# Moving state copies, routing's parts, the gate reduction and the first loads in the attention stage of a fused kernel

## The chip, the cores and the metric

The kernel runs on one core of a Trainium2 chip. A core has five engines, each with its own instruction queue that runs in order: TensorE (PE; its weight loads are shown as PEld), VectorE (DVE), ScalarE (ACT), GpSimd (POOL) and SyncE (SP, which only issues transfers here). Transfers run on 16 DMA engines. The metric is device time in microseconds from the first to the last instruction of one execution, with what lies around it; lower is better.

## The reference, cut to what matters

Three blocks follow one another on B = 4 sequences of S = 576 rows of 512 numbers: a retention (causal attention with a decay per head and no softmax), a mixture of eight experts with one expert for each row, and a Fourier block with a feed-forward part.

```python
ret = (q @ k.T) / 8 * Dmat            # Dmat = gamma_h ** (row - column), causal
x = ret @ v                           # (4, 576, 512), eight heads of 64
logits = x @ w_gate                   # (4, 576, 8)
local = sigmoid(x @ w_local)          # under 0.5, or at row 0: take the row's own argmax, else keep the last expert
out[b, s] = p[e] * (relu(x[b, s] @ w1[e]) @ w2[e])
u = x + real(fft2(x)); out = u + relu(norm(u) @ w_ch1) @ w_ch2
```

## The kernel before, in words

The change lies in the first stage, `attention`, and in two places of `fused_kernel` and `layouts` that feed it. The rows are cut into 18 steps (`STEPS`): for each of four blocks of 128 rows (c = 0 to 3) the four sequences one after the other, so step i = 4c + b, and then two steps for the last 64 rows of two sequences each (c = 4). All engines run an order that is written out by hand: the order of the Python calls is the order of each engine's queue.

What belongs to one step:

- `load(i)`: two transfers on SP's queue, q and k transposed (`qk`, 512 KB) and k and v (`vk`, 512 KB). There are three `qk` buffers and four `vk` buffers, so `load(i + 3)`, issued in step i, waits for the last reader of `qk(i)`.
- `prep(i)`, issued in step i - 2, on POOL: `qg`, q times its decay (c > 0), then `ks`, k times its decay (c < 4; two buffers).
- `scores(i)`: TensorE's state products `sp` from `ks` and v (c < 4; one PSUM bank, `st`); VectorE copies them into `total` (c = 0) or adds the earlier state; with c = 3 ScalarE copies the sum into `apart` in two halves (`sb`). Then TensorE's scores `a`, and VectorE's two products with the decay table `dec`, which make `am`.
- `outputs(i)`, in step i + 1: TensorE's products of state and `qg`, and of v and `am`, into `o`; ScalarE copies them to `xT`.
- `back(i)`, in step i + 1: TensorE multiplies `xT` by `idw`, the identity with the nine gate columns, into the one bank `tr`. VectorE sums the gates' part over the four blocks (`L`, L527). ScalarE takes the sum of magnitudes (`Abs`, L536, with a read-out), VectorE makes a scale of it in three small operations (L537 to L546), ScalarE writes the scaled row's fp16 high half (`xh`, L547), VectorE the low half (`xl`, L549). The bank is then free for the next `tr`.
- `route(c)`: for each block of four steps, a generator of four parts: maximum, differences `ls`, choice, and ScalarE's exponential `ex`; then a transposition, the normaliser (`rate`, L582 to L585) and a scan along the rows; then the choice turned back; then ranks by TensorE, the gate, and the slots at which rows go to their expert. `turn` advances every live generator once a step. After the last part, `scatter` sends rows by an indirect transfer on POOL's queue, two a step.
- `beside(i)`: work on the weights of expert 0, whose eight pieces `w.load(j)` brings (512 KB each, issued by `hook`): `absmax(j)` on ScalarE in step j + 6, `high(j)` on ScalarE and `low(j)` on VectorE in steps 11 and later.

A step's calls in order: `outputs(i - 1)`, first part of `beside`, `scores(i)`, `tr` and gates, second part of `beside`, `Abs` to `xh`, third part of `beside`, `prep(i + 2)`, `load(i + 3)`, `level` (the decay table of the next block, every fourth step), `turn`, `xl`, `scatter`, the first part of a new `route` (i = 4, 8, 12, 16), `hook`. After step 17 come the first half of an expert's products, the last routing, the scatter of the last rows, and the loads of the second expert's weights, whose number the routing has just found.

Of the kernel before, what the change touches and what calls it, by code (L numbers as in the profile page):

```python
# [20 lines left out]
E, FF = 8, 2048  # L21
# [20 lines left out]
WARM = 15  # L42
FILLED = 4
# [302 lines left out]
def attention(keep, tc, nc, A, xs, rows, hook, beside, after, sizes, zeros, first, spare, hid0, mt0):  # L346
# [19 lines left out]
    def load(i):  # L366
# [61 lines left out]
    def prep(i):  # L428
# [4 lines left out]
        if c > 0:  # L433
            qg = wk.tile([128, 4, 128], FP32, tag="qg", name="qg", bufs=3)
            for j in range(len(lanes)):
                w = slice(n * j, n * j + n)
                nc.gpsimd.tensor_tensor(out=qg[:, :, w], in0=qT[:, :, w], in1=qds[c][:, :, 0:n], op=ALU.mult)
        if c < 4:
            ks = wk.tile([128, 512], FP32, tag="ks", name="ks")
            h8 = lambda t: t.rearrange("p (h d) -> p h d", h=H)  # L440
            nc.gpsimd.tensor_tensor(
                out=h8(ks), in0=h8(k), in1=kd[:, c, :].unsqueeze(2).to_broadcast([128, H, D]), op=ALU.mult
            )
        pre[i] = (qg, ks)

    def scores(i):
# [27 lines left out]
        pair = [p2.tile([128, 4, 128], FP32, tag="a", name="a") for _ in range(2)]  # L474
        for j in range(len(lanes)):
            w = slice(n * j, n * j + n)
            for p in range(4):
                for g, a in enumerate(pair):
                    r = slice(64 * g, 64 * g + 64)
                    nc.tensor.matmul(out=a[w, p, 0:n], lhsT=kT[r, p, w], rhs=qT[r, p, w], start=True, stop=True)  # L480
        for g, a in enumerate(pair):
            for j in range(len(lanes)):
                w = slice(n * j, n * j + n)
                V.tensor_tensor(out=m[w, g::2, 0:n], in0=a[w, :, 0:n], in1=dec[w, g::2, w], op=ALU.mult)
# [33 lines left out]
    def back(i):  # L518
# [6 lines left out]
        if i % 4 == 0:  # L525
            L[c] = rt.tile([128, 4, 9], FP32, tag="L", name="L", bufs=2)
        V.tensor_reduce(  # L527
            out=L[c][:, i % 4, :], in_=tr[:, :, 128:137].rearrange("p a e -> p e a"), axis=AX.X, op=ALU.add
        )
# [6 lines left out]
        nc.scalar.activation(out=xh.bitcast(BF16), in_=tr, func=ACTF.Abs, accum_out=mx[:, 0:1])  # L536
        V.tensor_scalar(  # L537
# [8 lines left out]
        V.reciprocal(out=mx[:, 2:3], in_=pi)  # L546
        nc.scalar.activation(out=xh, in_=tr, func=ACTF.Copy, scale=mx[:, 2:3])  # L547
# [3 lines left out]
    def route(c):  # L551
# [89 lines left out]
        V.tensor_tensor(out=gate[:, at], in0=ps, in1=sm, op=ALU.mult)  # L641
        c8 = W("c8", [128, 2, 8])
# [77 lines left out]
    live = []  # L720

    def turn():
        for g in list(live):
            if next(g, "end") == "end":
                live.remove(g)

    level(1)
    for i in range(N):
# [7 lines left out]
        scores(i)  # L736
# [40 lines left out]
    next(early[3])  # L777
    next(r, None)
# [1439 lines left out]
def fused_kernel(tc, A, out, stop=None):  # L2218
    nc = tc.nc
    with ExitStack() as ctx:  # L2220
# [5 lines left out]
        with tc.manual_schedule():  # L2226
# [51 lines left out]
            def hook(i):  # L2278
                w = weights(0)
                if i == 0:  # L2280
# [12 lines left out]
                if 2 <= i < 10:  # L2293
                    w.load(i - 2)
# [69 lines left out]
def layouts(q, k, v, moe_w_gate, moe_w_local, moe_w1, moe_w2, moe2_w_ch1, moe2_w_ch2):  # L2364
# [3 lines left out]
    for i, lanes in enumerate(STEPS):  # L2368
# [10 lines left out]
        "w_gate": c(moe_w_gate),  # L2379
        "w_local": c(moe_w_local),  # L2380
# [24 lines left out]
```

## Time and profile before

| | |
|---|---|
| runs shown | 790.6, 798.08, 790.78 us; median 790.78 |
| profiled execution | 787.88 us, span 785.7 us |
| busy in the span | PE 724.8 (92%), PEld 542.8, DVE 592.3 (75%), ACT 411.8 (52%), POOL 126.8 us |
| DMA | 142.27 MB, mean 181 GB/s |
| mean granted clock of TensorE | 0.988 |
| attention's steps | from 7.7 to about 112 us |

Times in the rows below count from the span's start. A line such as L524 is a line of the kernel before. In a timeline, "[1.58 <-ACT xT L516]" says that the engine stood idle for 1.58 us before the instruction, and what ended that. A busy engine need not be the one that sets the end: within a stage, what counts is which wait ends last.

### The profile page before, as it was taken

The numbers are of one execution on the slowest core, as the hardware profiler recorded it, in microseconds if no ns is written. First come the engines' busy times: TensorE is split into PE (matmuls) and PEld (weight loads), VectorE is DVE, ScalarE is ACT, GpSimd is POOL, SyncE is SP. The second block draws the span as 40 slices with busy tenths as digits, with TensorE's granted clock in tenths as the row PEclk, the third lists the DMA queues.
The fourth block names the chain that finished last, engine by engine and source line by source line (L and its number), as shares of the span: only waits on it lengthen the run. The fifth ranks groups of instructions, "written<-read, shape, count | busy, mean of one in ns | idle before, by whom it ended". The sixth has DMA issues, their size and how long they took to land. (4 is left out here: it accounts for less than half of the span.)

```text
span 785.7 us, 17150 instructions
## 1 busy us (share of the span) xinstructions
PE 724.8 (92%) x6529; PEld 542.8 (69%) x6529; DVE 592.3 (75%) x1432; ACT 411.8 (52%) x829; POOL 126.8 (16%) x225
## 2 busy tenths in 40 slices
PE   8888898899999998879998999899899999999996
PEld 5677685655566555557644448778788888888885
DVE  3678888589889988857898969958876695646462
ACT  1356657378888797845847526426332451414140
POOL 3566443002102201113000011010010001010101
PEclk9999999899999999999999999999999999999998
DMA  9998449999998998964427276600550017110000
GB/s 296 355 305 293 154 115 309 295 315 344 293 360 304 270 352 287 262 235 149 136 77 240 102 214 232 175 28 2 170 150 2 28 62 195 28 55 2 28 2 27
DMA packets 91929, 142.27 MB, mean 181 GB/s; under 512 B 48116, under 2 KB 49017, under 8 KB 90814
## 3 DMA queue, kind: packets, MB, share of 16 engines
q1 hardware_dynamic: 87246, 126.78, 51.4%
q0 software_dynamic: 4592, 14.31, 5.0%
q8 instruction: 53, 0.87, 0.4%
q14 instruction: 38, 0.31, 0.1%
HBM read 97.55 MB, written 35.12 MB: 169 GB/s over the span
## 5 line engine op out<-in xcount | busy, mean ns | idle before, releaser
L1666 PE MATMUL g<-gxt,wh 128*128 128x256 f16 (+1 forms) x992 | 143.6, 284 | 2.6 <-DMA gxt<-un 1.4
L2011 PEld LDWEIGHTS <-hd 128*128 128x128 f16 x1176 | 114.2, 98 | 26.9 <-issue 7.1
L1666 PEld LDWEIGHTS <-wh 128*128 128x128 f16 x1056 | 102.8, 98 | 28.5 <-issue 4.9
L286 DVE SCALAR_TENSOR_TENSOR wl<-wst,ws,wh 128x1024 f16<-128x1024 f32 (+1 forms) x82 | 100.3, 1253 | 8.1 <-ACT wh L281 8.0
L281 ACT ACTIVATE wh<-wst,ws 128x1024 f16<-128x1024 f32 x80 | 89.0, 1140 | 26.1 <-DVE ws L274 25.7
L815 PE MATMUL ps<-xt,wh 128*128 128x320 f16 (+4 forms) x544 | 79.1, 284 | 8.1 <-DMA xt<-xs 5.8
L845 PE MATMUL ps<-wh,hid 128*128 128x512 f16 (+2 forms) x528 | 84.6, 302 | 0.2 <-ACT hid L831 0.2
L2011 PE MATMUL g<-wh,hd 128*128 128x256 f16 x448 | 78.3, 273 | 4.3 <-DVE u L2040 2.0
L1666 PE MATMUL g<-gxt,wl 128*128 128x256 f16 (+1 forms) x496 | 80.5, 285 | 0.0
L815 PEld LDWEIGHTS <-wh 128*128 128x128 f16 x640 | 57.5, 100 | 33.2 <-issue 13.8
L1872 POOL DMA_INDIRECT out<-u,orow x18 | 17.9, 993 | 383.9 <-DVE u L2040 284.8
L845 PEld LDWEIGHTS <-hid 128*128 128x128 f16 (+2 forms) x792 | 46.4, 100 | 42.4 <-issue 2.7
L239 ACT ACTIVATE wh<-wst 128x1024 bf16<-128x1024 f32 x66 | 69.3, 1050 | 7.7 <-DVE wst L311 5.2
L2040 DVE SCALAR_TENSOR_TENSOR u<-g,ffs,u 128x256 f32<-128x256 f32 (+1 forms) x63 | 34.1, 568 | 49.3 <-PE g L2011 48.7
L1982 DVE SCALAR_TENSOR_TENSOR s<-g,r 128x256 f32<-128x256 f32 x168 | 53.3, 374 | 23.4 <-ACT hd L1976 22.7
L1955 ACT ACTIVATE hd<-s 128x640 f16<-128x640 f32 x56 | 41.3, 737 | 47.8 <-DVE s L1982 47.8
L1975 ACT ACTIVATE r<-g 128x256 f32<-128x256 f32 x56 | 21.1, 378 | 84.0 <-PE g L1666 78.0
L2011 PE MATMUL g<-e,hd 128*128 128x256 f16 x504 | 59.9, 273 | 5.0 <-DVE u L2040 4.0
L859 POOL DMA_INDIRECT x<-y,mt x25 | 31.5, 1261 | 194.7 <-ACT y L857 149.7
L2011 PE MATMUL g<-wl,hd 128*128 128x256 f16 x224 | 61.1, 273 | 0.0
L1666 PEld LDWEIGHTS <-wl 128*128 128x128 f16 x528 | 51.9, 98 | 11.7 <-issue 1.1
L845 PE MATMUL ps<-wl,hid 128*128 128x512 f16 (+2 forms) x264 | 56.4, 302 | 0.0
(299 smaller groups left out, 1280.7 us busy)
## 6 DMA issues: line engine op xcount, KB each, us to landing
wst<-in_moe_w SPq DMA_DIRECT2D x64, 512.0 KB
raw<-in_ch SPq DMA_DIRECT2D x14, 1024.0 KB
qk<-in_qkv SPq DMA_DIRECT2D x18, 512.0 KB
vk<-in_qkv SPq DMA_DIRECT2D x16, 512.0 KB
pair<-ch SPq DMA_DIRECT2D x32, 256.0 KB
ch<-d SPq DMA_DIRECT2D x14, 512.0 KB
wst<-ch SPq DMA_DIRECT2D x14, 512.0 KB
u<-u SPq DMA_DIRECT2D x9, 512.0 KB
```

Of the source, the lines that this page charges most:

```text
L239: self.nc.scalar.activation(out=x, in_=t, func=ACTF.Abs, accum_out=self.am[:, j : j + 1])
L281: self.nc.scalar.activation(out=self.dst[0][:, j, :], in_=self.pieces[j], func=ACTF.Copy, scale=self.by(j))
L286: self.nc.vector.scalar_tensor_tensor(out=l[:, j, c], in0=self.pieces[j][:, c], scalar=self.by(j), in1=h[:, j, c], op0=ALU.mult, op1=ALU.s ...
L815: nc.tensor.matmul(out=ps, lhsT=m[:, k, 128 * f : 128 * f + 128], rhs=xt[:, x + k, :], start=(k == 0 and i == 0), stop=(k == 3 and i == last),
L845: nc.tensor.matmul(out=ps[r * j : r * j + r, 0:d], lhsT=hid[x][:, f, 128 * t : 128 * t + r], rhs=m[:, 4 + f // 2, c : c + d], start=(f == ...
L859: nc.gpsimd.indirect_dma_start(out=x2[:, :].rearrange("t (k d) -> (t k) d", k=k), out_offset=bass.IndirectOffsetOnAxis(ap=mt, axis=0), in_ ...
L1666: nc.tensor.matmul(out=ps, lhsT=m[:, k + 4 * (f // 8), 128 * (f % 8) : 128 * (f % 8) + 128], rhs=xt[x][:, k, :], start=(k == 0 and i == 0) ...
L1955: nc.scalar.activation(out=hd[:, 0, 2:7], in_=s, func=ACTF.Copy, scale=C2 / 2)
L1975: nc.scalar.activation(out=r, in_=p[:, 1:3], func=ACTF.Relu)
L1982: V.scalar_tensor_tensor(out=d, in0=x, scalar=0.0, in1=y, op0=ALU.max, op1=op)
L2011: nc.tensor.matmul(out=ps, lhsT=hid[k][:, y, x, :], rhs=E[w][m][k], start=(k == 0 and m == y == 0), stop=(k == 7 and y == 1),)
L2040: V.scalar_tensor_tensor(out=y, in0=p, scalar=fs[:, c : c + 1], in1=y, op0=ALU.mult, op1=ALU.add)
```

## The change

- `scores`: the scores `a` and `am` come first, then `sp`; the copy of the state (c = 0) goes from VectorE to ScalarE and, with the `sb` copies, into `keep_state`, called behind the row's `xh`.
- `back`: the gates' reduction comes behind `Abs` (but for the last row), and `xh` becomes a part of its own, behind the third part of `beside`.
- `route`: the first part (c < 3) runs in the following step behind its scores; the second and fourth part are cut in two (c < 3) by `yield "amid"`, and what follows the cut runs behind `xl`.
- `prep`: `ks` ahead of `qg`.
- Loads: `kd` between the halves of load 0; `idn` and one array `gates` (for `w_gate` and `w_local`) ahead of load 1, and `idw` made by a copy on ScalarE instead of a broadcast transfer; `cb`, `rt` and `pos` in step 1; `level` a step earlier; the zero fill in step 3 instead of 0 and the pieces of expert 0 in steps 4 to 11 instead of 2 to 9.
- `WARM` 15 to 9, `FILLED` 4 to 5.

The diff, cut to its core:

```diff
-WARM = 15
-FILLED = 4
+WARM = 9
+FILLED = 5
...
-    load(0)
-    kd = const("kd", [128, 4, 8], src=A["kd"].rearrange("p (c h) -> p c h", c=4))
+    kd = const("kd", [128, 4, 8])
+    load(0, lambda: nc.sync.dma_start(out=kd, in_=A["kd"].rearrange("p (c h) -> p c h", c=4)))
     dec = const("dec", [128, H, 128], src=A["dec"].rearrange("p (h q) -> p h q", h=H))
+    idw, idn = const("idw", [128, 4, 137]), keep.tile([128, 128], FP32, name="idn")
+    nc.sync.dma_start(out=idn, in_=A["idn"])
+    nc.sync.dma_start(out=idw[:, :, 128:137], in_=A["gates"].rearrange("p (c e) -> p c e", c=4))
+    nc.scalar.copy(out=idw[:, :, 0:128], in_=idn.unsqueeze(1).to_broadcast([128, 4, 128]))
     load(1)
...
-    idw = const("idw", [128, 4, 137])
-    nc.sync.dma_start(out=idw[:, :, 0:128], in_=A["idn"].unsqueeze(1).to_broadcast([128, 4, 128]))
-    nc.sync.dma_start(out=idw[:, :, 128:136], in_=A["w_gate"].rearrange("(c p) e -> p c e", p=128))
-    nc.sync.dma_start(out=idw[:, :, 136:137], in_=A["w_local"].rearrange("(c p) e -> p c e", p=128))
...
+    def rest():
+        for t, n in ((cb, "cb"), (rtab, "rt"), (pos, "pos")):
+            nc.sync.dma_start(out=t, in_=A[n])
...
-            if c == 0:
-                V.tensor_copy(out=total[b][0], in_=sp)
-            else:
+            if c > 0:
                 V.tensor_tensor(out=total[b][c % 2], in0=sp, in1=total[b][(c - 1) % 2], op=ALU.add)
-            if c == 3:
-                for g in range(2):
+            def keep_state():
+                if c == 0:
+                    nc.scalar.copy(out=total[b][0], in_=sp)
+                for g in range(2) if c == 3 else ():
                     r = slice(64 * g, 64 * g + 64)
                     nc.scalar.copy(out=apart[b][r, :, r], in_=total[b][1][r])
...
         nc.scalar.activation(out=xh.bitcast(BF16), in_=tr, func=ACTF.Abs, accum_out=mx[:, 0:1])
+        if i < N - 1:
+            logits()
...
         V.reciprocal(out=mx[:, 2:3], in_=pi)
+        yield
         nc.scalar.activation(out=xh, in_=tr, func=ACTF.Copy, scale=mx[:, 2:3])
...
         if c < 4:
             rate()
+        if c < 3:
+            yield "amid"
...
         V.tensor_tensor(out=gate[:, at], in0=ps, in1=sm, op=ALU.mult)
+        if c < 3:
+            yield "amid"
...
-        scores(i)
+        kept = scores(i)
+        for g in fresh:
+            next(g)
+        live.extend(fresh)
+        fresh.clear()
...
         next(r, None)
         next(more, None)
+        next(r, None)
+        kept()
         if i + 2 < N:
             prep(i + 2)
         if i + 3 < N:
             load(i + 3)
-        if i % 4 == 1 and 2 <= i // 4 + 2 <= 4:
-            level(i // 4 + 2)
+        if i % 4 == 0 and i < 16:
+            level(i // 4 + 1)
+        if i == 1:
+            rest()
         turn()
         next(r, None)
+        turn(amid)
+        amid.clear()
...
-            live.append(route(i // 4 - 1))
-            next(live[-1])
+            if i < 16:
+                fresh.append(route(i // 4 - 1))
+            else:
+                live.append(route(i // 4 - 1))
+                next(live[-1])
...
-                if i == 0:
+                if i == 3:
...
-                if 2 <= i < 10:
-                    w.load(i - 2)
+                if 4 <= i < 12:
+                    w.load(i - 4)
```

## Rows read from the trace of the kernel before

**Rows 1.** Stages: length; busy PE, PEld, DVE, ACT, POOL; clock, DMA share, GB/s

```profile
13.74:28.94 15.20, 12.78 (x171) 10.68 (x169) 8.89 (x24) 5.56 (x12) 4.39 (x4) 1.00 0.99 304
28.94:35.33 6.39, 4.81 (x75) 4.24 (x73) 4.51 (x12) 2.08 (x5) 4.29 (x4) 1.00 1.03 419
35.33:41.47 6.14, 4.96 (x74) 4.36 (x74) 5.11 (x18) 2.90 (x6) 2.86 (x4) 1.00 1.02 373
41.47:51.43 9.96, 9.88 (x153) 8.89 (x153) 7.17 (x29) 5.85 (x12) 4.88 (x7) 1.00 0.96 324
51.43:57.24 5.81, 4.78 (x73) 4.22 (x73) 4.03 (x14) 2.17 (x7) 5.25 (x11) 1.00 0.86 255
57.24:63.95 6.71, 4.95 (x73) 4.35 (x74) 5.71 (x16) 3.89 (x8) 4.38 (x8) 1.00 1.01 396
68.77:98.74 29.97, 25.08 (x388) 22.05 (x386) 26.55 (x89) 20.73 (x41) 16.29 (x29) 1.00 0.54 165
98.74:112.07 13.33, 12.84 (x175) 11.30 (x176) 11.94 (x44) 7.39 (x15) 5.22 (x16) 1.00 0.41 122
```

**Rows 2.** Timeline, first steps: start, length, engine, line, operation, out<-in

```profile
1.79 5.13 PE L717 MATMUL warm<-z 128*128 128x512 f16 x15 [1.79 <-POOL z L2272]
...
10.94 1.04 POOL L441 TENSOR_TENSOR ks<-vk,c_kd 128x512 f32<-128x512 f32 x1 [3.31 <-DMA vk<-in_qkv]
```

**Rows 3.** Timeline around routing's first and second part, T4 and T5

```profile
33.23 1.26 POOL L437 TENSOR_TENSOR qg<-qk,qd 128x512 f32<-128x512 f32 x1 [1.41 <-DMA qk<-in_qkv]
33.42 1.12 DVE L560 TENSOR_TENSOR ls<-L,m 128x32 f32<-128x32 f32 x1
...
34.71 0.57 ACT L516 COPY xT<-o 128x512 f32<-128x512 f32 x1
...
35.33 1.21 PE L524 MATMUL tr<-c_idw,xT 128*128 128x137 f32 x8 [1.58 <-ACT xT L516]
...
41.47 1.18 PE L524 MATMUL tr<-c_idw,xT 128*128 128x137 f32 x8 [1.18 <-DVE xr L549]
```

**Rows 4.** Waits up to 115 us: us in total, times, the longest

```profile
ACT xr L536 <- DVE L L527: 25.5, 16, 3.1
...
ACT xT L516 <- PE o L509: 9.9, 1, 9.9
...
PE sp L458 <- POOL ks L441: 3.0, 3, 1.2
```

**Rows 5.** Groups of instructions up to 112 us: count, busy, mean ns, idle before

```profile
L484 DVE TENSOR_TENSOR am<-a,c_dec 128x512 f32<-128x512 f32 x32 | 20.5, 680 | 2.8 <-PE a L480 2.8
L549 DVE SCALAR_TENSOR_TENSOR xr<-tr,mx,xr 128x512 f16<-128x512 f32 x17 | 12.7, 747 | 7.2 <-ACT xr L547 7.1
L286 DVE SCALAR_TENSOR_TENSOR wl<-wst,ws,wh 128x1024 f16<-128x1024 f32 x4 | 5.1, 1278 | 0.0
L468 DVE TENSOR_TENSOR sum<-sp,sum 128x256 f32<-128x256 f32 x12 | 4.9, 412 | 0.1
...
L583 DVE TENSOR_SCALAR sm<-sm 128x4 f32<-128x4 f32 x4 | 3.1, 784 | 0.1
...
L565 DVE TENSOR_REDUCE fr<-t 128x4 f32<-128x32 f32 x4 | 0.7, 186 | 0.1
...
L547 ACT ACTIVATE xr<-tr,mx 128x512 f16<-128x512 f32 x17 | 11.7, 687 | 13.5 <-DVE mx L546 8.4 <-DVE oh L605 3.1 <-DVE sm L582 2.0
L536 ACT ACTIVATE xr<-tr 128x512 bf16<-128x512 f32 x17 | 10.2, 598 | 25.6 <-DVE L L527 25.5
...
L281 ACT ACTIVATE wh<-wst,ws 128x1024 f16<-128x1024 f32 x8 | 9.0, 1143 | 0.0
...
L472 ACT COPY sb<-sum 64x256 f32<-64x256 f32 x8 | 3.2, 401 | 1.4 <-DVE sum L468 1.3
```

**Rows 6.** Timeline: piece 7's magnitude; the second expert's loads

```profile
80.02 1.06 ACT L239 ACTIVATE wh<-wst 128x1024 bf16<-128x1024 f32 x1
...
116.47 3.75 SPq L229 DMA_DIRECT2D wst<-in_moe_w  x6
```

More of the change, by code (lines that the diff above doesn't have):

```diff
@@ L364, in attention, with load @@
     loads = {}
-    def load(i):
+    def load(i, amid=lambda: None):
         lanes = STEPS[i]
@@ L371, in load @@
         nc.sync.dma_start(out=qk.rearrange("p x c s -> p (x c s)"), in_=A["qkv"][i, :, 0:1024])
+        amid()
         nc.sync.dma_start(
@@ L432, in prep @@
         qg = ks = None
[L433 to L437, printed above, removed]
         if c < 4:
@@ L443, in prep @@
             )
+        if c > 0:
+            qg = wk.tile([128, 4, 128], FP32, tag="qg", name="qg", bufs=3)
+            for j in range(len(lanes)):
+                w = slice(n * j, n * j + n)
+                nc.gpsimd.tensor_tensor(out=qg[:, :, w], in0=qT[:, :, w], in1=qds[c][:, :, 0:n], op=ALU.mult)
         pre[i] = (qg, ks)
@@ L451, in scores @@
         am[i] = m = wk.tile([128, H, 128], FP32, tag="am", name="am")
+        pair = [p2.tile([128, 4, 128], FP32, tag="a", name="a") for _ in range(2)]
+        for j in range(len(lanes)):
+            w = slice(n * j, n * j + n)
+            for p in range(4):
+                for g, a in enumerate(pair):
+                    r = slice(64 * g, 64 * g + 64)
+                    nc.tensor.matmul(out=a[w, p, 0:n], lhsT=kT[r, p, w], rhs=qT[r, p, w], start=True, stop=True)
+        for g, a in enumerate(pair):
+            for j in range(len(lanes)):
+                w = slice(n * j, n * j + n)
+                V.tensor_tensor(out=m[w, g::2, 0:n], in0=a[w, :, 0:n], in1=dec[w, g::2, w], op=ALU.mult)
         b, c = lanes[0]
@@ L464, in scores @@
                 )
-            if c == 0:
-                V.tensor_copy(out=total[b][0], in_=sp)
-            else:
+            if c > 0:
                 V.tensor_tensor(out=total[b][c % 2], in0=sp, in1=total[b][(c - 1) % 2], op=ALU.add)
-            if c == 3:
-                for g in range(2):
+            def keep_state():
+                if c == 0:
+                    nc.scalar.copy(out=total[b][0], in_=sp)
+                for g in range(2) if c == 3 else ():
                     r = slice(64 * g, 64 * g + 64)
                     nc.scalar.copy(out=apart[b][r, :, r], in_=total[b][1][r])
[L474 to L484, printed above, removed]
+            return keep_state
+        return lambda: None
     def outputs(i):
@@ L526, in back, with logits @@
             L[c] = rt.tile([128, 4, 9], FP32, tag="L", name="L", bufs=2)
-        V.tensor_reduce(
-            out=L[c][:, i % 4, :], in_=tr[:, :, 128:137].rearrange("p a e -> p e a"), axis=AX.X, op=ALU.add
-        )
+        whole = tr
+        def logits():
+            V.tensor_reduce(
+                out=L[c][:, i % 4, :], in_=whole[:, :, 128:137].rearrange("p a e -> p e a"), axis=AX.X, op=ALU.add
+            )
+        if i == N - 1:
+            logits()
         yield
@@ L536, in back @@
         nc.scalar.activation(out=xh.bitcast(BF16), in_=tr, func=ACTF.Abs, accum_out=mx[:, 0:1])
+        if i < N - 1:
+            logits()
         V.tensor_scalar(
@@ L719, in attention, with turn @@
     prep(1)
[L720 to L724, printed above, removed]
+    live, fresh, amid = [], [], []
+    def turn(of=None):
+        for g in list(live if of is None else of):
+            said = next(g, "end")
+            if said == "end":
                 live.remove(g)
-    level(1)
+            if said == "amid":
+                amid.append(g)
     for i in range(N):
@@ L777, in attention @@
     next(early[3])
+    next(r, None)
     next(r, None)
@@ L2378, in layouts @@
         "qkv": qkv.reshape(len(STEPS), 128, 2048),
-        "w_gate": c(moe_w_gate),
-        "w_local": c(moe_w_local),
+        "gates": c(
+            np.concatenate([moe_w_gate, moe_w_local], axis=1).reshape(4, 128, E + 1).transpose(1, 0, 2).reshape(128, 4 * E + 4)
+        ),
         "moe_w1": c(moe_w1),
```

8 lines of the change are left out of this document (3 added, 5 removed).

## The prediction

> **What bounds the kernel now.** I read four views in this order: busy time by stage, the timeline of the first 115 us, the list of waits, and the groups of instructions with their mean times. The change touches only the attention stage. It consists of 18 steps, and I mark step i+1 by the start of the `tr` matmuls of row i, called T(i): T0 is 13.74, T3 28.94, T4 35.33, T5 41.47, T7 51.43, T8 57.24, T9 63.95, T10 68.77, T15 98.74, T17 112.07.
>
> The stage has three limits one after the other. Up to T4 the DMA engines are full (shares 0.99 and 1.03) while TensorE works 12.78 of 15.20 us [rows 1]; the matmuls `sp` wait for `ks`, 3.0 us in three waits, and `ks` waits for its load [rows 2, 4]. From T5 to T7 TensorE is full: 9.88 of 9.96 us, so about 4.9 us a step is its floor [rows 1]. Four other intervals lie above it: T3 to T4 6.39, T4 to T5 6.14, T7 to T8 5.81, T8 to T9 6.71 [rows 1]. All four are routing's. In the first and third, `ex` stands on ScalarE ahead of the copy `xT` and waits for VectorE's `ls`, so `tr` starts 1.58 us late, "ACT xT". In the second and fourth, routing's second part stands on VectorE ahead of the low part `xl`, and `tr`, whose only bank `xl` frees, starts 1.18 us late, "DVE xr" [rows 3]. From T10 to T15 (29.97 us for five steps) VectorE is busy 26.55 us: nearly full [rows 1]. So a removed wait is worth its length before T10 and little after it.
>
> What the stage gains reaches the end: the second expert's weight loads are issued at 116.47 [rows 6], after the routing has named that expert, and the DMA engines are at a share of 0.41 from T15 to T17 [rows 1], so no transfer begun earlier holds them. I pass gains on one for one.
>
> **The start.** `kd` goes between the two halves of load 0; `idn` (64 KB) and one merged `gates` transfer (18 KB) go ahead of load 1, and a 256 KB broadcast, `cb`, `rt`, `pos`, the first `qd` and the 1.1 MB of zero fill go behind load 3 or later. At the 304 GB/s of the stage [rows 1] the 82 KB put `ks(1)`, now at 10.94 [rows 2], off by 0.3 us, to 11.2. After it come 1.04 us of `ks` and some 0.7 us of `sp`; the scores `a` of step 1 no longer stand behind `sp`. T0 becomes 13.0. For steps 1 to 3 TensorE needs 12.78/3 = 4.26 us [rows 1] and some 0.2 of gaps. The new loop on ScalarE is as long: `xh` 0.69, the state copy now on ScalarE, 0.4 by its neighbour `sb`, `xT` 0.57, `tr` 1.2, `Abs` with its read-out 0.75, and 0.75 for VectorE's three small operations with their hand-overs [rows 3, 5], together 4.4. I take 4.53, so T3 = 13.0 + 13.6 = 26.6 against 28.94: **-2.3**. Loads do not prevent it: loads 0 to 4 with their constants are 6.1 MB, which at 304 GB/s are there at about 23, and `sp(4)` wants `ks` at 25. Bounds: 0 if the loads come as late as now, -3.0 at TensorE's 4.26.
>
> WARM 15 to 9: the fifteen ran 1.79 to 6.92 [rows 2], and nothing waits for the six; what could lose is the clock, at most the 2 us that the first `a`, `sp` and `o` would take longer. I take 0. The copy that makes `idw` lies on ScalarE before its first `xT`, where it idles 9.9 us [rows 4]. FILLED changes nothing: no row is ready before step 7. `rest` is 0.18 MB and its first reader is step 5. `level` one step earlier is wanted two steps later.
>
> **Steps 4 and 8.** Routing's first part leaves the end of the step and comes after the next scores. `xT` has nothing ahead of it, and the step falls to TensorE's 4.9: 6.39 - 4.9 and 5.81 - 4.9, **-2.4**. Bounds: 0 if `xT` finds another instruction ahead, -2.6 at 4.8.
>
> **Steps 5 and 9.** They now hold the first part (five operations of some 0.2 us [rows 5]), `ex`, the normaliser (`rate`, four operations), then `xl`, and only then the rest of the second part. Counted from `tr`: `am` ends at 0.7, `sum` at 1.1, the maximum at 1.3. Then `ls`, and here VectorE meets GpSimd: `ls` took 1.12 us, from 33.42 to 34.54, beside a `qg` that ran 33.23 to 34.49; and `L583` took 0.78 in the mean though it has four numbers a row [rows 3, 5]. In the new order `ks(i+2)` can begin when `sp(i)` has given its buffer back, at 0, and `qg` follows to 2.4. So `ls` ends at 2.4, `ex` at 2.7, `Abs` with its read-out at 3.45, the three small operations with hand-overs at 4.1, `xh` at 4.85, `xl` at 5.6, and the next `tr` at 5.8. 6.14 - 5.8 and 6.71 - 5.8: **-1.25**. Without a meeting `xl` ends at 4.65 and TensorE's 4.9 to 5.0 binds, -2.85; if `rate` meets both GpSimd operations too, 6.6, and the sum is +0.35.
>
> The Trainium skill says why (SBUF — State Buffer, "Who interferes with whom"): the second port pair is an exclusive lock, and whichever of a VectorE operation with two SBUF inputs and a GpSimd operation that reads SBUF starts first holds it to its end. The 1.12 us agrees. It speaks against moving the first part to where `qg` runs; by the rule alone the step is 5.8 and the sum the one below, without it 5.0 and 1.6 us less.
>
> **Gates behind magnitudes.** `Abs` now waits for the gates' reduction `L527`, 25.5 us in 16 waits [rows 4]. Reversed, it starts 0.2 us earlier, but the reduction then waits for `Abs` and stands ahead of the three small operations: 0. If it fitted inside the read-out, -0.2 for each of nine steps (1 to 3, 5, 9, 12 to 15), -1.8.
>
> **Steps 11 to 17.** In steps 12 to 15 the two `sb` copies (0.8 us) leave a gap ahead of `Abs` and go between `xh` and the next `xT`. The `high` of 1.14 us, which lay there, goes ahead of `xh`, into the 0.7 us that ScalarE waits for VectorE. That exchange alone is -0.3 a step. But VectorE is the bound, and its work is the same: `am` 1.36, `sum` 0.41, `low` 1.28, gates and small ones 0.7, `xl` 0.75 [rows 5], and routing's late parts now stand ahead of the next `am` rather than ahead of `xl`. Carrying each step on from the one before I get 5.2, 6.5, 6.05, 6.65 and 6.1 us for T10 to T15, 30.5 against 29.97, and 0.5 more for T15 to T17, because the routing's last part after step 15's `xl` delays `am(16)`: **+1.0**. The scatter of that part's rows waits for the slots, one `xl` later than now; the fetch behind it is wanted when the last `o` ends: **+0.5**. Bounds for both: -1.5 (only the exchange) and +3 (every `sb` pair fully on the path).
>
> **Later weights.** The eight pieces of expert 0 are loaded in steps 4 to 11 instead of 2 to 9, behind the zero fill, but `absmax(j)` stays at step j+6. It stands on ScalarE ahead of `Abs`; if the piece is late, `Abs`, `xh` and the next `xT` queue behind it and TensorE waits for `xT`. Up to piece 7 I count 24.0 MB (15 loads 15.7, constants 1.6, zeros 1.1, pieces 4.2, scattered rows 1.4). At 330 GB/s, between the rows' 304 and 373, they are there at 2.5 + 72.7 = 75. `absmax(7)`, now at 80.02 [rows 6], would be wanted at 80 - 6 = 74. A tie: **+0.5**.
>
> **The sum.** -2.3 - 2.4 - 1.25 + 1.0 + 0.5 + 0.5 = -3.95. The profiled execution took 787.88 us (span 785.7): 783.9. The median of the runs shown is 790.78, 2.9 above it: 790.78 - 3.95 = **786.8**.
>
> **The rivals.** (a) *The late part moves too*: no meeting in steps 5 and 9 (-2.85), steps 11 to 17 keep only the exchange (-1.5), start -2.3, steps 4 and 8 -2.4: -9.0, 781.8. For it: most of what VectorE idles from T10 to T15, 3.4 us, would be used. Against it: that share is already 0.89. (b) *Given back*: the start and steps 4 and 8 gain 4.7, but both GpSimd operations hit `rate` (+0.35) and all `sb` copies count (+3), with pieces late by 1.4: 0, 790.8. (c) *Slower*: the pieces of expert 0 become the bound. Where the 24.0 MB move at 290 GB/s, below the 304 of the first stage, piece 7 is there at 2.5 + 82.8 = 85.3, 5.3 after the 80.02 of now, and every step behind is that much later: +5.3, 796.1. It decides from 310 GB/s (landing at 80) down. Against it: 373 to 419 GB/s where only loads run [rows 1].
>
> **How the numbers follow.** Forecast 0.48, its own range 784.5 to 789; (a) 0.25; (b) 0.17; (c) 0.10. The range 781.5 to 792 leaves out the far end of (a) and most of (c). About 1%, 7.9 us, is what a measurement of this kernel tells from no change: faster by more takes nearly all of (a), 0.24; slower by more only the tail of (c) with a lost clock at the start, 0.06; within 0.70.
>
> **What would show it.** T3 near 26.6; `tr` of rows 4 and 8 without a wait for `xT`; T5 - T4 and T9 - T8 near 5.8 with an `ls` of about 1 us beside `qg`; T10 to T15 no shorter than now, with `xT` behind `sb`; `absmax(5)` to `absmax(7)` starting without a DMA wait. The forecast is wrong if T17 moves by more than 8 or less than 1 us, or if the stretch behind T17 changes its length.

## The result and the profile after

The changed kernel is slower: 796.97 us in the median against 791.92, ratio 1.0054 with a 95% interval of 1.0033 to 1.0076; taken a second time, 1.0065 (1.0035 to 1.0094). That is 4 to 5 us more, where 4 us less were forecast, and outside the range. The profiled execution took 798.7 us, span 796.5 us.

I count again by T(i), the start of `tr` of row i (L533 after, L524 before). "Again" is a second profile of the same changed kernel, "repaired" the kernel of the ninth experiment, explained below. T10 to T15 and T15 to T17 cover five and two steps.

| us | T0 | T3 | T3 to T4 | T4 to T5 | T7 to T8 | T8 to T9 | T10 to T15 | T15 to T17 | T17 |
|---|---|---|---|---|---|---|---|---|---|
| before | 13.74 | 28.94 | 6.39 | 6.14 | 5.81 | 6.71 | 29.97 | 13.33 | 112.07 |
| after | 14.94 | 28.04 | 4.89 | 9.72 | 4.89 | 7.72 | 33.78 | 15.33 | 119.52 |
| again | 15.36 | 28.45 | 4.89 | 6.21 | 4.89 | 7.80 | 32.73 | 15.52 | 115.65 |
| repaired | 13.85 | 26.95 | 4.89 | 6.21 | 4.89 | 6.10 | 30.31 | 13.72 | 108.21 |

Behind T17 the span is 673.6 us before, 677.0 and 677.3 in the two profiles of after, and between 673.2 and 678.1 in the experiments. There a longer end goes with no one edit. What lengthened it by 3.4 and 3.6 us in the two profiles of after is not shown; the prediction had taken it as fixed. The loss that can be explained lies before T17. Busy time by stage in the changed kernel, columns and stages as in [rows 1]:

```profile
14.94:28.04 13.10, 11.81 (x172) 10.21 (x168) 7.33 (x22) 6.38 (x15) 6.64 (x6) 1.00 0.95 316
28.04:32.93 4.89, 4.89 (x75) 4.22 (x73) 3.17 (x9) 1.87 (x4) 2.27 (x2) 1.00 0.96 267
32.93:42.65 9.72, 6.71 (x78) 5.75 (x74) 7.00 (x22) 3.08 (x7) 2.27 (x2) 0.82 0.70 268
42.65:52.78 10.13, 10.13 (x156) 8.84 (x152) 6.85 (x29) 6.01 (x13) 4.85 (x6) 1.00 0.84 285
52.78:57.67 4.89, 4.89 (x76) 4.22 (x72) 3.35 (x9) 1.92 (x5) 3.88 (x8) 1.00 0.89 258
57.67:65.39 7.72, 5.18 (x77) 4.33 (x74) 6.20 (x18) 4.16 (x9) 5.91 (x11) 1.00 1.01 374
70.41:104.19 33.78, 27.18 (x388) 23.36 (x386) 30.11 (x90) 21.70 (x41) 17.60 (x29) 0.95 0.51 173
104.19:119.52 15.33, 13.90 (x177) 11.87 (x176) 11.49 (x43) 6.63 (x15) 5.99 (x16) 0.89 0.37 106
```

Steps 4 and 8 are pure TensorE now (4.89 of 4.89 us). Steps 5 and 9 are not: TensorE works 6.71 and 5.18 us of 9.72 and 7.72, and VectorE, which now has routing's first part in these steps, is busy 7.00 and 6.20 us (5.11 and 5.71 before). The clock is below 1.00 in step 5 and in the last two rows. The list of TensorE's waits up to 112 us (waiting tile and line, what it waited for, us in total, times, the longest) names what holds it:

```profile
PE tr L533 <- ACT xT L525: 3.8, 2, 2.6
PE row L597 <- DVE cc L588: 3.0, 1, 3.0
...
PE tr L533 <- DVE kr L612: 1.8, 1, 1.8
PE row L597 <- DVE cc L586: 1.8, 2, 1.0
PE tr L533 <- ACT wh L239: 1.5, 1, 1.5
```

`row`, the transposition of routing's choice `cc`, waited 0.4 us once in the kernel before, for the last full block. Now it waits for blocks 0, 1 and 2, 3.0 us at worst, with `o`, `a`, `sp` and the next `tr` behind it in TensorE's queue. The timeline of step 5 shows why `cc` is late (start, length, engine, line, operation):

```profile
34.81 1.04 POOL L440 TENSOR_TENSOR ks<-vk,c_kd 128x512 f32<-128x512 f32 x1 [3.44 <-DMA vk<-in_qkv]
34.84 1.03 DVE L586 SCALAR_TENSOR_TENSOR cc<-L,fr 128x4 bf16<-128x4 f32 x1
...
35.81 1.26 POOL L447 TENSOR_TENSOR qg<-qk,qd 128x512 f32<-128x512 f32 x1
35.91 1.19 DVE L588 CAST cc<-fr 1x4 bf16<-1x4 f32 x1
...
37.15 0.22 PE L597 MATMUL row<-c_cb,cc 128*4 128x128 bf16 x1 [3.01 <-DVE cc L588]
...
37.30 1.97 PE L509 MATMUL o<-qg,sum 64*64 64x128 f32 x16
...
39.20 1.81 PE L518 MATMUL o<-am,vk 128*64 128x128 f32 x16
```

Two operations on four numbers a row take 1.03 and 1.19 us instead of 0.16 each, and end when GpSimd's `ks` and `qg` end. I call this a meeting: an operation of VectorE that stands still beside work of GpSimd. TensorE idles 3.01 us, and after that its clock is at the lower level for a while: `o` takes 1.97 and 1.81 us where 1.09 is its time at the higher. In step 9 the normaliser meets the same two products:

```profile
60.82 0.99 POOL L689 DMA_INDIRECT xs<-xr,c_slot_i  x1 [0.28 <-POOL xr L687]
...
61.77 2.40 DVE L602 TENSOR_SCALAR sm<-sm 128x4 f32<-128x4 f32 x1
...
61.88 1.03 POOL L440 TENSOR_TENSOR ks<-vk,c_kd 128x512 f32<-128x512 f32 x1
...
62.88 1.26 POOL L447 TENSOR_TENSOR qg<-qk,qd 128x512 f32<-128x512 f32 x1
...
64.50 0.74 DVE L568 SCALAR_TENSOR_TENSOR xr<-tr,mx,xr 128x512 f16<-128x512 f32 x1
...
65.39 0.82 PE L533 MATMUL tr<-c_idw,xT 128*128 128x137 f32 x5 [1.54 <-ACT wh L239]
```

L602 starts at 61.77, while GpSimd still issues the scatter of a row (L689), and ends at 64.17, when both products are over. Two such scatters stand ahead of `ks` in GpSimd's queue, so it begins 4.21 us behind T8 and reaches the normaliser. `xl`, and with it the only `tr` bank, is 2.2 us later. In the second profile the same operation took 2.50 us, and in step 13 L604 took 2.70 and 2.69.

The start: WARM's products end earlier than before, `ks(0)` begins at 8.68 instead of 6.58 and `ks(1)` at 13.17 instead of 10.94, and the first `o` runs at the low clock. SyncE issues the load that `ks(1)` waits for at 5.15, and at 3.13 in the kernel before. The rows that answer [rows 2]:

```profile
1.79 4.02 PE L740 MATMUL warm<-z 128*128 128x512 f16 x9 [1.79 <-POOL z L2311]
...
5.15 1.08 SPq L373 DMA_DIRECT2D vk<-in_qkv  x1
...
8.68 1.04 POOL L440 TENSOR_TENSOR ks<-vk,c_kd 128x512 f32<-128x512 f32 x1 [4.94 <-DMA vk<-in_qkv]
...
10.61 2.57 PE L518 MATMUL o<-am,vk 128*64 128x128 f32 x16
...
13.17 1.04 POOL L440 TENSOR_TENSOR ks<-vk,c_kd 128x512 f32<-128x512 f32 x1 [3.45 <-DMA vk<-in_qkv]
```

And in the kernel before:

```profile
3.13 0.65 SPq L372 DMA_DIRECT2D vk<-in_qkv  x1
...
6.58 1.04 POOL L441 TENSOR_TENSOR ks<-vk,c_kd 128x512 f32<-128x512 f32 x1 [2.85 <-DMA c_kd<-in_kd]
```

The end: the first expert products wait for the fetch (L708, the transfer that brings the scattered rows back, transposed) and run at the low clock, 1.04 us where four took 0.60 before, and the second expert's loads are 7.6 us later than in [rows 6]:

```profile
112.73 2.69 SPq L708 DMA_TRANSPOSE wh<-xs  x2
...
116.55 1.04 PE L854 MATMUL ps<-wh,wh 128*128 128x256 f16 x4 [1.43 <-DMA wh<-xs]
...
124.03 3.69 SPq L229 DMA_DIRECT2D wst<-in_moe_w  x6
```

### The profile page after: what moved, and what is told of

Its sections match the earlier page's. It is cut to its first block, busy times and chain, and to the rows that moved or that the text cites. A ratio compares the mean times of both kernels' runs of the same rounds, so it can differ in the third digit from the quotient of the medians.

```text
span 796.5 us, 17117 instructions
## 1 busy us (share of the span) xinstructions
PE 732.6 (92%) x6523; PEld 547.7 (69%) x6523; DVE 593.6 (75%) x1428; ACT 413.9 (52%) x834; POOL 129.5 (16%) x225
## 5 line engine op out<-in xcount | busy, mean ns | idle before, releaser
L2050 PE MATMUL g<-wh,hd 128*128 128x256 f16 x448 | 79.9, 276 | 4.3 <-DVE u L2079 2.0
L854 PEld LDWEIGHTS <-wh 128*128 128x128 f16 x640 | 57.4, 100 | 35.2 <-issue 15.3
```

Of the source, the lines that this page charges most:

```text
L854: nc.tensor.matmul(out=ps, lhsT=m[:, k, 128 * f : 128 * f + 128], rhs=xt[:, x + k, :], start=(k == 0 and i == 0), stop=(k == 3 and i == last),
L2050: nc.tensor.matmul(out=ps, lhsT=hid[k][:, y, x, :], rhs=E[w][m][k], start=(k == 0 and m == y == 0), stop=(k == 7 and y == 1),)
```

## The experiments

Four theories: *row* (the place of `row` in TensorE's queue), *port* (VectorE's small operations stand still beside GpSimd's products, after the port rule that the prediction names), *loads* (the new places of the zero fill and the weights), and *start and fetch* (the ends of the stage). All edits are to the changed kernel, except where said. The ratio is always to the kernel before. Intervals such as T4 to T5 are those of one profiled execution each.

**1. Routing's first part back at the end of its step.**

```diff
-            if i < 16:
-                fresh.append(route(i // 4 - 1))
-            else:
-                live.append(route(i // 4 - 1))
-                next(live[-1])
+            live.append(route(i // 4 - 1))
+            next(live[-1])
```

> The changed kernel with one part undone: routing's first part is again the last thing of steps 4, 8 and 12. Row theory (TensorE's transposition of the choice, `row`, follows `tr` in the same step as the choice is made and holds TensorE's queue until `cc` is there): T4 to T5 falls from 9.7 to about 6.2, T8 to T9 from 7.7 to about 6.7, T12 to T13 from 7.7 to about 6.5, while T3 to T4 and T7 to T8 rise from 4.9 to 6.4 and 5.8 because `ex` is ahead of `xT` again: net -3.5 us of the changed kernel's time. Late-load theory (zero fill and weights in new steps make `ks` wait for its load, and that is what holds step 5): T4 to T5 stays above 8.5, net +1 to +2. Start theory (the loss is before T0): net +1 to +2 as well.

Ratio 1.0032 (1.0001 to 1.0062). T4 to T5 is 5.03 and T12 to T13 6.55, as the row theory has it, but T7 to T8 is 7.48 and T8 to T9 7.87. Between T7 and T8 `ls` ran into both products:

```profile
52.99 1.03 POOL L440 TENSOR_TENSOR ks<-vk,c_kd 128x512 f32<-128x512 f32 x1
...
53.18 2.12 DVE L579 TENSOR_TENSOR ls<-L,m 128x32 f32<-128x32 f32 x1
...
53.99 1.25 POOL L447 TENSOR_TENSOR qg<-qk,qd 128x512 f32<-128x512 f32 x1
```

T8 to T9 missed the 6.7 of the row theory. So the meeting follows the part wherever it goes, and its place in TensorE's queue is not the whole cause.

**2. `row` one step behind the choice (blocks 0 and 1).**

```diff
-        live.extend(fresh)
-        fresh.clear()
+        if i > 9:
+            live.extend(fresh)
+            fresh.clear()
...
         turn()
+        live.extend(fresh)
+        fresh.clear()
         next(r, None)
```

> The changed kernel with routing's second part (`row`, the normaliser, the scan) of blocks 0 and 1 one step later than its first part; the first part stays behind the next scores. Row theory: nothing on TensorE waits for `cc` in steps 5 and 9, T4 to T5 falls from 9.7 to 5 to 6 with a clock of 1.00, T8 to T9 from 7.7 to 6 to 6.7 (`absmax` still waits for its piece), steps 6 and 10 take 5 to 6 and 5.6; T10 comes 5 us earlier; the time 4 to 6 us lower than the changed kernel's. Late-load theory: T4 to T5 stays above 8 and the time falls by less than 2.

Ratio 1.0061 (1.0032 to 1.0090): no gain. T4 to T5 fell to 5.33, as expected, but T8 to T9 only to 6.88, and the normaliser met the products one step later, L602 with 1.22 us in step 6 and 2.00 in step 10, where T9 to T10 became 6.52 instead of 5.02. The row theory had T4 to T5 right and the time wrong.

**3. WARM 15.**

```diff
-WARM = 9
+WARM = 15
```

> The changed kernel with WARM 15 again. Clock theory of the start (nine warming products end early, TensorE idles until `ks(0)`, and its clock is low when the first products come): the granted clock is 1.00 from 10 to 13.5 us, o(0) takes 1.1 to 1.5 instead of 2.57, T0 is 13.7 instead of 14.94, the time 1.2 us lower. Landing theory (the order of the first transfers makes `vk(0)` and with it `ks(0)` late): T0 stays within 0.3 of 14.94 whatever the clock.

The granted clock from 10 to 14 us is 1.00 (0.57 after), the first `o` takes 0.43 and 1.09 us in its two pieces, and T0 is 14.09, where the clock theory had 13.7. T0 was 14.94 to 15.78 in the seven profiles that have WARM 9 and the changed order of `a` and `sp` (mean 15.18), and 13.85 to 14.56 in the four with WARM 15 (mean 14.22): 1.0 us. But the clock is only a part of it. In the four, `sp` of step 1 waits for `ks(1)` and T0 comes 1.71 to 1.72 us behind the start of `ks(1)`; in the seven it is 1.71 to 2.49 behind, 0.3 us more in the mean. The other 0.6 us is an earlier `ks(1)`, 12.51 against 13.14 in the mean, with the load that it waits for; that WARM is the reason for that is not shown. The time did not show the gain: ratio 1.0072 (1.0048 to 1.0097). In the profile T8 to T9 was 8.28, with L602 at 2.82 us.

**4. Zero fill and pieces of expert 0 at their old steps.**

```diff
-                if i == 3:
+                if i == 0:
...
-                if 4 <= i < 12:
-                    w.load(i - 4)
+                if 2 <= i < 10:
+                    w.load(i - 2)
```

> The changed kernel with the zero fill in step 0 and the pieces of expert 0 in steps 2 to 9, as before. Late-load theory: `ks` of steps 5, 9 and 13 no longer waits for its load, T4 to T5 falls from 9.7 to below 7, `absmax` of 7 waits for nothing (T8 to T9 -1.3), the time 3 to 5 us lower than the changed kernel's. Row theory: T4 to T5 stays above 8.5 because `row` still stands behind `cc`; only T8 to T9 gets 1.3 shorter, and T3 comes 1 to 2 us later because the early loads share with the zero fill: the time within 1.5 us of the changed kernel's.

Ratio 1.0054 (1.0019 to 1.0089). `absmax` did not hold T9 any more, and T8 to T9 was still 7.63, now behind VectorE, with L602 at 2.33 us. The load theory falls as a cause of the time. Its one hit, T4 to T5 below 7 (6.96), says nothing, since the changed kernel had 6.21 there without any edit (experiment 8).

**5. `sp` ahead of `a`, `qg` ahead of `ks` again.** In `prep` the block of `qg` goes ahead of that of `ks`; in `scores`:

```diff
-        pair = [p2.tile([128, 4, 128], FP32, tag="a", name="a") for _ in range(2)]
...
         b, c = lanes[0]
         if c < 4:
             sp = p1.tile([128, 4, 64], FP32, tag="st", name="sp")
...
+        pair = [p2.tile([128, 4, 128], FP32, tag="a", name="a") for _ in range(2)]
```

> The changed kernel with the old order inside a step: state products `sp` ahead of the scores `a`, and `qg` ahead of `ks`. Port theory (VectorE's operations on four numbers a row in routing stand still while GpSimd's `ks` and `qg` run, and `ks`, freed by `sp` at the end of TensorE's step, now begins just when they do): `ks` starts 1.1 us earlier in the step, the choice meets one product instead of two, no VectorE operation of routing takes above 1.3 us, T4 to T5 about 6, T8 to T9 about 6.7, T12 to T13 about 6.7: 2 to 3 us less than the changed kernel. Theory that only the place of the transposition `row` counts: the intervals stay within 0.5 of 6.2 to 9.7, 7.7 and 7.7. T0 to T3 longer by up to 2 us, because `sp` waits for `ks` again.

Ratio 1.0115 (1.0070 to 1.0160), the slowest of all. The port theory expected shorter meetings and was wrong in that: L604 (here the normaliser's second operation) took 2.40 and L606 2.69 us, and T8 to T9 and T12 to T13 stayed at 7.99 and 7.68. T0 went to 17.75 and each step up to T3 to 5.46 instead of 4.37. So `a` ahead of `sp` is a gain at the start, and with `qg` first the meetings were no shorter; the two orders were not tried apart.

**6. The fourth part of block 2 not cut.**

```diff
         V.tensor_tensor(out=gate[:, at], in0=ps, in1=sm, op=ALU.mult)
-        if c < 3:
+        if c < 2:
             yield "amid"
```

> The changed kernel, but routing's fourth part of block 2 is not cut: its slots come ahead of `xl` in step 15, as before. Fetch theory (the last four steps are longer by 2.5 us because the four scatters behind these slots and the transposing fetch behind them are later, TensorE waits 1.4 us for the fetched rows, and its clock is low in the first expert products after that wait): the fetch is issued 1.5 to 2 us earlier relative to T15, the first expert products do not wait, they take 0.60 for four instead of 1.04, T16 to T17 is 6.6 instead of 9.0: the time 2.4 us less than the changed kernel's. Otherwise (the stretch is longer because ScalarE and VectorE are fuller): T16 to T17 stays above 8.5 and the time is the same.

Fetch theory: T16 to T17 fell from 9.01 to 7.12 and T15 to T17 to 13.40, the fetch was issued 7.58 us behind T15 instead of 8.54 and 9.34, and the first products ran at the higher clock:

```profile
114.62 0.61 PE L854 MATMUL ps<-wh,wh 128*128 128x256 f16 x4
...
116.22 0.60 PE L854 MATMUL ps<-wh,wh 128*128 128x256 f16 x4 [0.55 <-DMA wh<-xs]
```

Ratio 1.0040 (1.0011 to 1.0068); its difference to the changed kernel, some 2 us, is inside the intervals. The profiles are clearer: T15 to T17 is 13.40 to 13.91 in the four kernels of the changed order with the uncut part, and 15.33 to 16.23 in the eight profiles with the cut one.

**7. GpSimd's products of steps 5, 9 and 13 held until the normaliser is done.**

```diff
+        if i in (5, 9, 13):
+            hold = rt.tile([128, 1], FP32, tag="hold", name="hold")
+            nc.gpsimd.tensor_copy(out=hold, in_=last["sm"][:, 0:1])
+            prep(i + 2)
         next(r, None)
```

> The changed kernel, but in steps 5, 9 and 13 GpSimd takes up `ks` and `qg` only when VectorE has finished the normaliser (it first copies one column of it). Port theory: no operation of the choice or the normaliser takes above 0.3 us, `row` waits 0.3 us at most for `cc`, T4 to T5 is 5 to 5.6, T8 to T9 6 to 6.5 (`absmax` and its piece remain), T12 to T13 5.8 to 6.3, in all 3 to 6 us less than the changed kernel. Theory that the order on TensorE alone is to blame: the first part's chain is long without any meeting, `row` still waits 1 us or more, and these three intervals lose less than 1 us each. Late-load theory: nothing changes in T4 to T5, since GpSimd's products there were late by their load anyway.

Ratio 0.9995 (0.9970 to 1.0020): 790.74 us where the changed kernel beside it took 795.16, so this one cause is worth 4.4 us, as much as the whole loss, and the intervals of the two do not overlap. No operation of the choice or the normaliser takes above 0.25 us in these steps; step 9:

```profile
59.09 0.17 DVE L602 TENSOR_SCALAR sm<-sm 128x4 f32<-128x4 f32 x1
...
59.74 0.18 POOL L786 COPY hold<-sm 128x1 f32<-128x1 f32 x1 [0.52 <-DVE sm L604]
...
59.88 1.03 POOL L440 TENSOR_TENSOR ks<-vk,c_kd 128x512 f32<-128x512 f32 x1
...
61.10 1.09 PE L533 MATMUL tr<-c_idw,xT 128*128 128x137 f32 x7
```

T8 to T9 is 6.09 and T13 to T14 5.57 (7.60 after). T12 to T13 is 7.23, not the 5.8 to 6.3 expected: the granted clock there is 0.76, and the two parts of `o` take 1.97 and 1.54 us instead of 1.09 each. T4 to T5 is 6.21 without any meeting, not the 5 to 5.6 expected: `row` still waited 1.1 us there and 1.0 in step 9.

**8. The changed kernel again.** No edit.

> The changed kernel itself, once more, to see which of its intervals repeat. Port theory: T8 to T9 and T12 to T13 are again near 7.7, with a normaliser operation of 2.3 to 2.8 us in each; T4 to T5 depends on when `ks` gets its load and lies between 6 and 9.7. Start theory: T0 again 14.9 with a low clock from 10 to 13.5 us. Fetch theory: T16 to T17 again about 9.

T8 to T9 7.80 and T12 to T13 7.68 repeat, and so does T0. T4 to T5 is 6.21, not 9.72: here `ks` began at 35.69, 2.35 us behind T4 and after `cc`; in the first profile it began 1.88 us behind T4 and caught `cc`. The normaliser met the products instead, and cost this step nothing:

```profile
36.39 0.36 DVE L602 TENSOR_SCALAR sm<-sm 128x4 f32<-128x4 f32 x1
...
36.69 1.27 POOL L447 TENSOR_TENSOR qg<-qk,qd 128x512 f32<-128x512 f32 x1
36.79 0.18 DVE L603 RECIPROCAL sm<-sm 128x4 f32<-128x4 f32 x1
```

L602 was freed at the end of `ks` (36.73), though `qg` had begun. The loads decide that by half a microsecond, and the step pays 3.5 for it (9.58 in the sixth experiment, 8.75 in the fifth).

**9. Three repairs at once:** WARM 15, the uncut part, and the held products (the edits of 3, 6 and 7).

> The changed kernel with three repairs at once: WARM 15 again, the fourth part of routing's block 2 not cut, and GpSimd's `ks` and `qg` of steps 5, 9 and 13 held until the normaliser is done. If the three causes are separate and their sizes add (1.1 us at T0 with WARM 15, 1.9 in T16 to T17 with the uncut part, 4 to 5 with the held products), T17 comes at about 110 against 112.07 before the change, and the time is 6 to 8 us below the changed kernel's and 2 to 3 below the time before. If they share one bottleneck (expert 0's weights or VectorE from step 11 on), the gains overlap: T17 stays at 112 to 113 and the time at that of before.

Ratio 0.9934 (0.9910 to 0.9959), 786.83 against 791.97 us: faster than both kernels. The three gains do not stand in each other's way: T17 is 108.21, 3.9 us ahead of before, where 110 was expected if they add.

**10. The three repairs, and `sb` of block 3 straight behind its sum.**

```diff
+            if c == 3:
+                keep_state()
+            else:
+                return keep_state
```

> The kernel with the three repairs, and with the pair of `sb` copies of block 3 straight behind their sum again (ahead of `Abs` instead of between `xh` and the next `xT`). Exchange theory (the pair is on the path in its new place): the waits of `tr` for `xT` at T12, T14 and T15 (0.5 to 2.5 us) shrink by 0.8 each, T11 to T15 falls from 25.3 to about 23.5 to 24.4, the time 1 to 2 us lower. Theory that VectorE alone bounds these steps: `Abs` starts later by what `xT` starts earlier, T11 to T15 stays within 0.5 of 25.3 and the time the same.

Ratio 0.9958 (0.9930 to 0.9987), not better than without. `tr` no longer waits for `xT` at T12 but 1.77 us for `xl` instead of 1.37 for `xT`, and T11 to T15 is 25.78 against 24.99. The exchange theory found no support: `xT` behind `sb` waits beside a chain on VectorE that is as long.

**11. The kernel before, with the hold of experiment 7 alone.**

> The kernel before with one edit: in steps 5, 9 and 13 GpSimd takes up `qg` and `ks` only when the normaliser is done. Port theory: L583 took 1.77 us beside them in step 9 and 0.60 in steps 5 and 13; it takes 0.2 in all three, T8 to T9 falls from 6.71 to about 5.2, T4 to T5 and T12 to T13 by 0.4 to 0.9; the time 1.5 to 3 us lower. Theory that the meeting costs only the changed order anything: the intervals stay within 0.3 and the time the same.

Ratio 0.9977 (0.9951 to 1.0004), unclear. T8 to T9 went from 6.71 to 5.10 and T12 to T13 from 6.48 to 5.48, so the meeting cost the old order 1.0 to 1.6 us a time as well. But three intervals grew. T4 to T5 went from 6.14 to 6.86, where 0.4 to 0.9 less was expected. T6 to T7 went from 5.15 to 6.55, and T10 to T11 from 5.60 to 6.49: the products that were put off met the ranks' part two steps later. T15 to T17 went from 13.33 to 14.99, with a wait of 0.65 us ahead of the first expert products and the low clock behind it, 1.04 and 1.06 us for four. In steps 6 and 7:

```profile
48.29 1.27 POOL L437 TENSOR_TENSOR qg<-qk,qd 128x512 f32<-128x512 f32 x1 [3.86 <-DMA qk<-in_qkv]
...
48.79 0.80 DVE L636 TENSOR_TENSOR ohs<-oh,c_cb 128x32 bf16<-128x32 bf16 x1
...
50.78 1.04 POOL L441 TENSOR_TENSOR ks<-vk,c_kd 128x512 f32<-128x512 f32 x1 [1.22 <-DMA vk<-in_qkv]
50.90 0.94 DVE L651 TENSOR_TENSOR carry<-carry,c 128x2 bf16<-128x2 bf16 x1
```

**12. The three repairs with `row` one step later** (the edit of 2, products held in steps 6, 10 and 13).

> The kernel with the three repairs, and routing's second part of blocks 0 and 1 one step behind its first part; GpSimd's products are held in steps 6, 10 and 13. Row theory without any meeting in the way: in the three repairs' kernel `row` still waits 1.1 us for `cc` in step 5 and 1.0 in step 9, and the steps take 6.21 and 6.10; here nothing on TensorE waits there, T4 to T5 and T8 to T9 fall to 4.9 to 5.3, steps 6 and 10 stay below 5.3, T10 comes 1.5 to 2.3 us earlier and the time is 1 to 2 us below that of the three repairs. Other outcome: expert 0's pieces are not there earlier, `absmax` waits for them by what the steps gained, T10 stays within 0.5 and the time the same; then `row` was on the path only by place, and the weights would be next.

Ratio 0.9937 (0.9911 to 0.9964), the same as the three repairs, and T4 to T10 takes 32.3 us in both. The waits of TensorE for `cc` in steps 5 and 9 are gone, and `tr` waits for `xl` in their place:

```profile
38.62 1.18 PE L533 MATMUL tr<-c_idw,xT 128*128 128x137 f32 x8 [1.12 <-DVE xr L568]
59.85 1.18 PE L533 MATMUL tr<-c_idw,xT 128*128 128x137 f32 x8 [1.13 <-DVE xr L568]
```

In step 5 that is a meeting again (`ks` was not held there; `cc` took 0.69 and 1.19 us). In step 9 there is none: `absmax` stands behind `ex`, `ex` behind the first part, and `Abs`, `xh` and `xl` behind `absmax`. This chain is as long as TensorE's wait for `cc`. Neither of the outcomes that I had written down says so.

## Why the prediction was wrong, point by point

**Steps 4 and 8: right.** -2.4 forecast, 6.39 and 5.81 became 4.89 each, -2.4; no `tr` there waits for `xT`.

**Steps 5 and 9: the step that failed.** The sum had 5.8 a step, -1.25 together. Measured is +1.2 in one profile and +4.6 in the other. Two terms of it were wrong. *The step without a meeting* was put at TensorE's 4.9 to 5.0. It is 6.09 and 6.21 (experiment 7). I counted the first part's chain up to `xl`, but not the instruction that reads its result: `row` stands on TensorE directly behind `tr` and waits 1.0 to 1.1 us for `cc`. Experiment 12 adds that this wait is not alone; taken away, an equal chain by `ex`, `absmax` and `Abs` is next in step 9. *The meeting* was put at one product, by the `ls` of 1.12 us that [rows 3] show, and two products were kept as a bound of 6.6. It was also put in the wrong place: `ks` was to begin with the step and `qg` to hold `ls`, but `ls` took 0.19 us in steps 5 and 9 of both profiles. `ks` began 1.88 and 2.35 us behind T4, when its load was there, and 4.21 and 4.29 behind T8, when GpSimd was done with two scatters, which the prediction had not counted. So the meeting fell on `cc` or on the normaliser, and there it lasted over both products: 2.40 and 2.50 us in step 9, 2.70 and 2.69 in step 13. L583's mean of 784 ns [rows 5] hid that the old order had such a case. Its single durations are 0.60, 1.77, 0.59 and 0.17 us, and the long one stands beside both products:

```profile
59.65 1.26 POOL L437 TENSOR_TENSOR qg<-qk,qd 128x512 f32<-128x512 f32 x1
...
60.16 1.77 DVE L583 TENSOR_SCALAR sm<-sm 128x4 f32<-128x4 f32 x1
...
60.87 1.03 POOL L441 TENSOR_TENSOR ks<-vk,c_kd 128x512 f32<-128x512 f32 x1
```

The rule of the Trainium skill that the prediction weighed (SBUF — State Buffer, "Who interferes with whom": the port pair is held for a whole instruction, and the other one is blocked) fits what was seen, and removing the overlap gave the 4.4 us back; that it is the port, and not something else that the two engines share, no run here separates. In the trace here the block often lasts longer than one instruction: over two products, 2.3 to 2.8 us.

It does not always. In step 5 of the first profile L586 was freed at the end of `ks`. Over all fourteen profiles, an operation of routing caught where one product follows the other was held over both sixteen times. Each time GpSimd had come to the first product without a wait, in twelve of them from a scatter. It was freed between the two at least thirteen times where GpSimd had waited before the first product, and three times where the first product itself took 1.10 to 1.55 us. Why is open, and so is what the scatters have in it: no run moved them away from the products.

**The lost clock** had no term in these steps. In the first profile it adds 1.6 us to step 5: `o` 1.97 and 1.81 us instead of 1.09 each, after TensorE had idled 3.01 us. With the 1.9 us by which `row` waits longer than in the second profile (3.01 against 1.11) that is the 3.5 us between them.

**The start: right in kind, mis-sized.** T3 was to be 26.6 and is 28.04 and 28.45: -0.9 and -0.5 instead of -2.3. The step of 4.37 is even better than the 4.53 forecast; T0 is what failed, 14.94 and 15.36 instead of 13.0. The chain behind `ks(1)` was right, 1.04 and 0.7 us forecast, 1.77 and 2.14 measured from its start to T0; `ks(1)` itself, put at 11.2, began at 13.17 and 13.22. It began at 12.13 to 13.40 in the twelve profiles with the new order of the first loads and at 10.94 and 11.21 in the two with the old. I had counted the 82 KB ahead of load 1 and not the issuing: SyncE gave out the load of `vk(1)` at 4.49 to 5.46 us, 3.13 and 3.29 in the old order. `ks(0)` is late too, at 7.31 to 8.78 against 6.58 and 6.66. That it is the issuing is argued from these times; which of the moved transfers makes them late was not tried. The clock with the six warming products gone, taken at 0 with a loss of at most 2 us, cost some 0.3 us of T0 in the mean (experiment 3).

**Gates behind magnitudes: 0**, not tried alone. `Abs` no longer waits for the reduction, and steps 1 to 3 run at 4.37.

**Steps 11 to 15: +0.5 forecast, +3.8 and +2.8 measured** (33.78 and 32.73 us against 29.97). The count for T10 to T15, 30.5, is what these steps take without the meeting: 30.3 to 31.3 in experiments 7, 9, 10 and 12. The meeting of step 13 was not in it, though it is the same one as in step 9; its delay goes on into step 14 (T12 to T14 15.3 us in both profiles, 12.4 to 13.4 with the products held). `xT` does stand behind `sb`, as forecast, for 0.5 to 1.4 us in the kernels without a meeting, but that is no cost by itself (experiment 10).

**Steps 16 and 17 and the fetch: +0.5 each forecast, 2.0 and 2.2 in all measured.** I had the fetch wanted when the last `o` ends and one `xl` late. It was issued 0.9 and 1.7 us later behind T15 than before, the expert products waited 1.43 and 1.06 us for it, and after that wait they ran at the low clock for the most part. Experiment 6 gave 1.9 us of T15 to T17 back.

**The later weights: +0.5 forecast, 0 in effect beside the meetings.** `absmax` waits for a piece, 1.32 us in step 9, but with the old places T8 to T9 was no shorter (7.63, experiment 4). With the meetings gone the old places were not tried. So rival (c), the late pieces, named a time near the measured one, 796.1, and is wrong; the agreement is chance. Rival (b) is the one that came true in kind: steps 4 and 8 gain, and the normaliser gives it back beside both products. Its price, 0, lacked `row`, step 13, the fetch and the clock.

In the first profile the terms add up to T17 7.45 us later than before, in the second to 3.58. The repaired kernel shows what is left when the meetings, the cut part and WARM 9 are taken out: T3 -2.0, steps 4 and 8 -2.4, steps 5 and 9 -0.5, T10 to T15 +0.3, T15 to T17 +0.4, and 0.4 in the steps between, together -3.9 at T17, and 5 us of the time.

## What to carry to other kernels

Before moving a chain of small VectorE operations, list what GpSimd runs in its new place, and count in its queue what stands ahead of the products too (here loads and scatters), since that sets where the meeting falls. Price it by a whole back-to-back run of GpSimd's work as the bound, not by one instruction; if it cannot be moved away, let GpSimd wait for one of the chain's results, and look at where its work lands then (it cost 1.4 us two steps on in experiment 11). Then ask of each result of the moved chain which in-order queue reads it first: here it was TensorE's, with the whole step behind it. And a part of a chain that is put off at one place makes every later reader late: follow the slots as far as the fetch. Of a transfer that is put ahead of another, count the issuing as well as the bytes.

## What the runs showed of the hardware that I had not expected

- An operation on four numbers a row (0.16 to 0.18 us) took up to 2.82 us beside the end of a scatter and two GpSimd products that start 1.00 us apart. TENSOR_SCALAR, TENSOR_TENSOR, SCALAR_TENSOR_TENSOR and CAST were all seen to stand still. RECIPROCAL was not: L603 kept 0.18 us inside `qg` (36.79, experiment 8). Nor was TENSOR_REDUCE, L601 with 0.17 us inside `ks` (36.19 there), nor `xl`, which reads an operand in PSUM. In the changed kernel it starts inside `qg` and keeps its 0.75 us:

```profile
69.16 1.27 POOL L447 TENSOR_TENSOR qg<-qk,qd 128x512 f32<-128x512 f32 x1
...
69.51 0.75 DVE L568 SCALAR_TENSOR_TENSOR xr<-tr,mx,xr 128x512 f16<-128x512 f32 x1 [0.73 <-ACT xr L566]
```

- Half a microsecond in when a load lands (`ks` 1.88 or 2.35 us behind T4) made a step of 9.72 or 6.21 us.
- The length of one wait did not tell whether the clock would fall. Behind waits of 1.06 and 1.43 us ahead of the first expert products the granted clock was 0.68 and 0.60 over 4 us. With 0.55 us in experiment 6 it stayed at 1.00, but in experiment 11 the products ran at the lower level behind 0.65 us. Waits of 1.37 and 0.75 us around T12 left the next step at 0.76 in experiment 7 (`o` 1.97 and 1.54 us) and at 1.00 in experiment 9 (1.09 each).
